# The conversion phase of a fused attention and two-MLP kernel: 298 steps in another order, 20 of them with another engine or pass

## Chip, core and metric

One NeuronCore of a Trainium2 chip runs the whole program. The metric is the device time of one execution in microseconds, the median of the runs shown. The engines are PE (TensorE: matmuls, and PEld, its weight loads), DVE (VectorE), ACT (ScalarE), POOL (GpSimd) and SP (SyncE, which here only issues DMAs). Each takes its instructions in order.

## What is computed

The reference, cut to what matters:

```python
# q, k, v: (8, 8, 576, 64), p: (8, 8, 32, 64), all float32
def sm_attn(qq, kk, vv):
    s = scale * qq @ kk.T; s -= max(s); a = exp(s); return (a / sum(a)) @ vv
p_packed = sm_attn(p, k, v)                 # 32 packed queries per head
x = sm_attn(q, p_packed, p_packed)          # back to 576 tokens per head
x = x.transpose(0, 2, 1, 3).reshape(4608, 512)
h = x @ w_in;  x = (h * sigmoid(1.702 * h)) @ w_out          # 512 -> 2048 -> 512
g = x @ w_gate; x = (g * sigmoid(g) * (x @ w_val)) @ w_out2  # 512 -> 1536 -> 512
```

The five weight matrices arrive as 64-bit floats; everything else is 32-bit. The result has to keep the accuracy of 32-bit floats, so matmul operands are split into a high part and a rest (type fp32r), and each product is three matmuls (`mm3`: high by high, high by rest, rest by high).

## The kernel before

The work goes batch by batch. In each batch the attention's second product is folded into the first MLP: `do_z` multiplies the packed values by `w_in` into `z`, `p1` (L216 through `mm3`, `h<-a,z`) multiplies `z` by the attention weights `a2`, `act1` and `act2` apply the activation and split its result into `gh`, and `p2` (`acc<-gh,wo`) multiplies by `w_out`. One unit is one of 16 column blocks of one half batch: `p1 n`, `act1 n`, `act2 n`, `p2 n`. There are 256 units. After them comes the second MLP.

The change is in the first 19 units. There the weights of the first MLP have to be converted too: 16 blocks of `w_in` (`in 0` to `in 15`) and 16 of `w_out` (`out 0` to `out 15`), each 128 x 512. One block goes through these steps:

- `stage` (L282): SP issues the DMA of a block's 64-bit words, 512 KB, into a buffer that later holds a converted block, so it has to wait until that buffer is free.
- `rebias` (L188): ACT reads the high words as floats and rescales them into `f` (tile `w32`, three buffers).
- `to_f32` (L193): a first pass takes the top bits of the low words into `c` (ACT, L197), and two DVE passes (L199, L201) put sign, exponent and mantissa together. Both read two tensors from SBUF.
- `split_w` or `split_out` (L478, L304, by `split` at L204): ACT rounds to the high part (L205), then POOL or DVE subtracts it from the whole (L206), which frees `f`. The engine is the step's last word; without one it is POOL. `split_w` then has ACT issue a DMA that stores the block to `win`, from where later batches load it. Its buffers are of tag `wh` (three), or, for odd blocks above 4, of tag `raw` (three), which the loads of q and k (`load_raw`) use too.

`do_z n` needs two blocks of `w_in`, `p2` of unit n the block `out` n (modulo 16).

The order in which all this is issued is the text `FIRST` (L19): 298 steps, parted by semicolons, with batch 0's attention (`do_T`, `sc1`, `max1`, `exp1`, `norm1`, `a1T`, `pv`, `do_D`, `sc2`, `max2`, `exp2`, `norm2`, and `split_*` of their results) and, marked `+`, the start of batch 1's. `issue` (L851) calls one function per step. The framework in which the kernel is written takes this order as priority: an engine's instructions may leave it where something later is ready earlier. From unit 19 on a loop issues `p1`, `act2`, `act1`, `p2` of each unit, and the texts `SECOND` and `STEADY` what stands between.

Of the kernel before, what the change touches and what calls it, by code (L numbers as in the profile page):

```python
# [19 lines left out]
    load_raw 0; load_p 0; stage in 0; make_consts; load_raw 1; stage in 2; stage in 1; load_raw 2; load_v 0 0;  # L20
    stage in 3; load_v 0 1; do_p; split_p; do_T 0 0; split_T 0 0; do_T 0 1; split_T 0 1 dve; rebias in 0;
    do_T 1 0; do_T 1 1; sc1 0; load_raw 3; to_f32 in 0; stage in 5; rebias in 2; max1 0; exp1 0; rebias in 1;
    split_T 1 0 dve; split_T 1 1 dve; split_w 0 dve; stage in 4; sc1 1; max1 1; exp1 1; do_T 2 0; do_T 2 1;
    norm1 0; a1T 0; to_f32 in 1; rebias in 3; stage out 0; to_f32 in 2; split_w 2 dve; split_T 2 0 dve;
    copy_a1T 0; split_w 1 dve; pv 0; norm1 1; do_D 0; split_F 0; split_D 0; rebias in 5; to_f32 in 3; split_T 2 1; a1T 1;
    do_T 3 0; stage out 1; rebias out 0; do_T 3 1; split_T 3 0 dve; split_T 3 1 dve; to_f32 in 5; split_w 3;
    stage in 7; copy_a1T 1; sc2 0 0; rebias in 4; to_f32 out 0; pv 1; do_D 1 act; split_F 1; split_D 1; max2 0 0; sc2 1 0;
    exp2 0 0; norm2 0 0; split_w 5 dve; split_a2 0 0; max2 1 0; do_z 0; exp2 1 0; norm2 1 0; stage in 6;
    split_a2 1 0 dve; do_z 1; to_f32 in 4; stage in 8; rebias out 1; split_w 4; stage out 2; to_f32 out 1;
    split_out 0; p1 0; act1 0; rebias in 7; rebias in 6; split_out 1; stage in 13; sc2 0 1; do_z 2; stage in 9;  # L30
    p1 1; act2 0 pool; to_f32 in 7; max2 0 1; split_w 7; sc2 1 1; act1 1; stage out 12; rebias out 2;
    to_f32 in 6; exp2 0 1; norm2 0 1; stage out 3; to_f32 out 2; rebias in 8; split_w 6; stage in 10; do_z 3;
    p1 2; act2 1; stage out 4; rebias in 9; act1 2; rebias out 4; split_out 2; split_a2 0 1; stage in 11;
    to_f32 in 8; max2 1 1; exp2 1 1; rebias out 3; to_f32 in 9; p1 3; split_w 8; stage in 15; rebias in 10;
    to_f32 out 4; act2 2 pool; act1 3; split_out 4 dve; p2 0; split_w 9; stage in 12; to_f32 out 3; do_z 4;
    to_f32 in 10; split_out 3; p1 5; act2 3 pool; rebias in 11; p1 4; act1 4; act1 5; rebias in 13; norm2 1 1;
    p2 1; to_f32 in 11; rebias in 15; split_w 10; stage out 5; split_w 11; to_f32 in 13; do_z 5; stage in 14;
    to_f32 in 15; split_a2 1 1 dve; act2 4 pool; rebias in 12; p2 2; to_f32 in 12; stage out 6; rebias out 5;
    split_w 15; p1 6; act2 5; split_w 12; load_v 1 1; stage out 7; p2 3; to_f32 out 5; rebias in 14; split_w 13;
    act1 6; do_z 6; p1 7; rebias out 7; load_p 1; split_out 5 dve; to_f32 in 14; stage out 8; act2 6 pool;  # L40
    act1 7; rebias out 6; rebias out 8; split_w 14; p1 9; p2 5; p1 8; load_v 1 0; to_f32 out 6; do_z 7;
    stage out 9; act2 7; act1 8; stage out 10; to_f32 out 7; stage out 11; rebias out 12; split_out 6 dve;
    rebias out 9; to_f32 out 8; to_f32 out 9; rebias out 10; to_f32 out 12; p2 4; p2 6; stage out 13;
# [66 lines left out]
def kernel(  # L110
# [856 lines left out]
```

## Time and profile before

| | |
|---|---|
| median of 3 runs | 1714.39 us (1714.21 to 1720.82) |
| profiled execution | 1722.94 us |
| its span, first to last instruction | 1721.2 us |
| PE busy | 1645.1 us (96%) |
| DVE busy | 1209.8 us (70%) |
| ACT busy | 777.3 us (45%) |
| POOL busy | 309.5 us (18%) |
| mean granted TensorE clock | 0.977 |

A row of the profile names the engine, the line of the kernel, the operation and out<-in by the program's tile names, with buffer numbers left out. `<-` after a bracket or between two names is "waited for". Since `split` is a helper, its ACT cast is always L205 and its subtraction L206; the tile tells them apart (`wh`: blocks of `w_in`; `wo`: of `w_out`; `gh`: a unit's activation; `a`: attention weights).

### The profile page before, as it was taken

Reading aid. Unit: us, or ns where it says so; the run is one execution under the profiler, and the core shown is the slowest. Engines: PE = TensorE matmul, PEld = TensorE weight load, DVE = VectorE, ACT = ScalarE, POOL = GpSimd, SP = SyncE. Lnnn points to the kernel's source line nnn. Section 1 sums busy time; section 2 is a strip of 40 time slices with the busy share of each in tenths; the row PEclk is TensorE's granted clock in tenths of the full one; section 3 lists DMA queues with packets and bytes.
Section 4 is the critical chain, followed back from the end, with each engine's and each line's share of the span. In section 5 each row is a group of like instructions: output and inputs, shape, how many; then the busy total and the mean of one; then the engine's idle time right before and its main releaser. Section 6 shows DMA issues by size and latency. Waiting matters only on the chain.

```text
span 1721.2 us, 25917 instructions
## 1 busy us (share of the span) xinstructions
PE 1645.1 (96%) x9264; PEld 1465.1 (85%) x9264; DVE 1209.8 (70%) x2268; ACT 777.3 (45%) x1611; POOL 309.5 (18%) x252
## 2 busy tenths in 40 slices
PE   5678999999999999999999999999999999999998
PEld 4558899998999899999998888888888888888887
DVE  6887978887787977878589555674658466756662
ACT  4675656656465565656455322242224222322222
POOL 1444313222131221302012111000100001001010
PEclk7789999999999999999999999999999999999999
DMA  8864665646466563624388754443445354425411
GB/s 237 266 233 123 197 200 179 218 147 209 129 199 185 163 225 117 212 74 163 125 290 301 265 174 137 163 147 124 157 145 166 95 176 155 154 80 165 157 49 49
DMA packets 169344, 290.59 MB, mean 169 GB/s; under 512 B 54784, under 2 KB 96768, under 8 KB 169216
## 3 DMA queue, kind: packets, MB, share of 16 engines
q1 hardware_dynamic: 165760, 280.03, 50.5%
q10 hardware_dynamic: 3456, 8.91, 1.4%
q8 instruction: 73, 1.20, 0.3%
q14 instruction: 55, 0.45, 0.1%
HBM read 230.16 MB, written 58.72 MB: 168 GB/s over the span
## 4 chain that ended last, share of the span: by engine, by line
PE 73%; DVE 7%; issue 7%; DMA 3%; ACT 2%; POOL 2%; SPq 0%; DVEq 0%; POOLq 0%; ACTq 0%
PE acc L216 31%; PE gv L216 29%; PE h L216 8%; PE pv L400 2%; PE sc L216 2%; PE zp L504 2%; DVE z L507 2%; DMA wh<-win 2%; DVE gh L206 1%; DVE g L554 1%; POOL wo L206 1%; DVE T L335 0%; DMA x<-x2d 0%; PE a1T L383 0%; POOL Th L206 0%
## 5 line engine op out<-in xcount | busy, mean ns | idle before, releaser
L216 PE MATMUL gv<-xh,w 128*128 128x512 f32 x2304 | 554.5, 389 | 0.0
L216 PEld LDWEIGHTS gv<-xh,w 128*128 128x128 f32 x2304 | 432.4, 188 | 89.7
L216 PE MATMUL acc<-gh,wo 128*128 128x288 f32 x3072 | 463.8, 299 | 12.7 <-POOL wo L206 3.1
L216 PEld LDWEIGHTS acc<-gh,wo 128*128 128x128 f32 x3072 | 432.1, 192 | 17.8 <-POOL wo L206 4.0
L216 PE MATMUL acc<-wo,gh 128*128 128x512 f32 x1296 | 326.9, 389 | 0.4
L216 PEld LDWEIGHTS acc<-wo,gh 128*128 128x128 f32 x1296 | 243.0, 188 | 52.1 <-DVE c L210 1.7
L216 PE MATMUL h<-a,z 128*128 128x288 f32 x1536 | 257.0, 301 | 6.2 <-DVE g L554 3.4
L206 DVE TENSOR_TENSOR gh<-g,gh 128x288 fp32r<-128x288 f32 (+1 forms) x293 | 181.2, 618 | 88.6 <-ACT gh L205 87.1
L216 PEld LDWEIGHTS h<-a,z 128*128 128x128 f32 x1536 | 227.1, 193 | 16.5 <-DVE g L554 5.7
L205 ACT CAST gh<-g 128x288 fp32r<-128x288 f32 (+1 forms) x304 | 140.2, 462 | 178.8 <-DVE g L554 130.5
L206 POOL TENSOR_TENSOR gh<-s,gh 128x512 fp32r<-128x512 f32 x60 | 83.0, 1384 | 699.4 <-ACT gh L205 644.7
L798 DVE TENSOR_TENSOR c<-gv,c 128x512 f32<-128x512 f32 x192 | 132.3, 689 | 84.0 <-ACT tb L813 56.6
L205 ACT CAST gh<-s 128x512 fp32r<-128x512 f32 x60 | 37.3, 621 | 247.3 <-DVE s L809 229.5
L552 ACT ACTIVATE sig<-h 128x288 f32<-128x288 f32 x256 | 104.5, 409 | 94.9 <-PE h L216 91.8
L554 DVE SCALAR_TENSOR_TENSOR g<-sig,h 128x288 f32<-128x288 f32 x256 | 114.0, 446 | 36.3 <-ACT sig L552 33.3
L798 DVE TENSOR_TENSOR ta<-gv,c 128x512 f32<-128x512 f32 x96 | 66.2, 689 | 83.1 <-PE gv L216 83.1
L509 POOL TENSOR_TENSOR z<-z,z 128x512 fp32r<-128x512 f32 x56 | 74.7, 1335 | 178.0 <-ACT z L508 178.0
L507 DVE TENSOR_TENSOR z<-zp,z 64x512 f32<-64x512 f32 x112 | 77.0, 688 | 22.5 <-ACT z L506 19.2
L504 PE MATMUL zp<-wh,E 128*128 128x512 f32 x224 | 67.3, 409 | 16.2 <-DMA wh<-win 9.7
L818 ACT ACTIVATE s<-c 128x512 f32<-128x512 f32 x48 | 30.4, 633 | 95.9 <-DVE c L798 95.9
L506 ACT COPY z<-zp 64x512 f32<-64x512 f32 x112 | 65.2, 582 | 14.3 <-PE zp L504 12.1
L206 POOL TENSOR_TENSOR Th<-T,Th 128x576 fp32r<-128x576 f32 x30 | 46.0, 1543 | 126.3 <-ACT Th L205 125.3
(128 smaller groups left out, 1610.0 us busy)
## 6 DMA issues: line engine op xcount, KB each, us to landing
w<-w2s SPq DMA_DIRECT2D x144, 512.0 KB, 3.3
wh<-win SPq DMA_DIRECT2D x112, 512.0 KB, 4.3
w2s<-w SPq DMA_DIRECT2D x36, 512.0 KB, 3.8
w<-w2s SPq DMA_DIRECT2D x48, 256.0 KB, 2.7
raw<-in_k_dram SPq DMA_DIRECT2D x64, 144.0 KB, 3.7
raw<-in_q_dram SPq DMA_DIRECT2D x64, 144.0 KB, 3.7
x2d<-x SPq DMA_DIRECT2D x16, 576.0 KB, 3.8
w2d<-f SPq DMA_DIRECT2D x36, 256.0 KB, 3.2
```

Source lines behind the costliest of these rows:

```text
L205: ACT.copy(dst[:, 0], src)
L206: eng.tensor_tensor(out=dst[:, 1], in0=src, in1=dst[:, 0].bitcast(F32), op=ALU.subtract)
L216: PE.matmul(o, lhsT=lhs(a), rhs=rhs(c), start=first and n == 0, stop=last and n == 2)
L400: PE.matmul(ps[:, c].rearrange("p h i -> p (h i)"), lhsT=vv[:n, k, 2 * c:2 * c + 2].rearrange("p h d -> p (h d)"), rhs=st["a1T", g][:n, k, ...
L504: PE.matmul(ps, lhsT=E[:, c].rearrange("p a i -> p (a i)"), rhs=w[c][:, d], start=d == 0, stop=d == 1)
L506: ACT.copy(x[o], ps[r])
L507: DVE.tensor_tensor(out=x[o], in0=ps[o], in1=x[o], op=ALU.add)
L509: POOL.tensor_tensor(out=y[:, 1], in0=x, in1=y[:, 0].bitcast(F32), op=ALU.subtract)
L552: ACT.activation(s, ps[:, :HS], AF.Tanh, scale=0.5 * 1.702)
L554: DVE.scalar_tensor_tensor(out=g, in0=s, scalar=1.0, in1=ps[:, :HS], op0=ALU.add, op1=ALU.mult)
L798: DVE.tensor_tensor(out=o, in0=ps, in1=c, op=ALU.add)
L818: ACT.activation(s2, c2, AF.Tanh, scale=0.5)
```

## The change

The text `FIRST` is replaced. It holds the same 298 steps in another order, and 20 of them name another engine:

- from POOL to DVE: `split_w` 3, 9, 11, 12, 13, 14; `split_out` 1, 9, 13, 14; `act2` 0, 4, 6;
- from DVE to POOL: `act2` 1 and `split_a2 1 0`;
- the first pass of `to_f32` from ACT to DVE: `in` 2, 11, 14, 15 and `out` 0.

For the last of these `to_f32` gets an engine: on DVE the first pass is a logical right shift of the low word by 29. Of the steps that move furthest: `load_p 0` goes ahead of `load_raw 0`; `stage out 3` goes 21 steps ahead, `stage in 12` 21, `p1 8` 18 (ahead of `do_z 6`), `load_raw 4` 14, `load_raw 5` 9, `+do_p` 20, `+do_T 0 0` 21, `+do_T 1 0` 19; `load_v 1 0` goes 21 back, `p1 12` 18, `p2 6` 13. The texts `SECOND` and `STEADY` and all that follows stay.

The diff:

```diff
@@ -17,39 +17,40 @@
 
 
 FIRST = """
-    load_raw 0; load_p 0; stage in 0; make_consts; load_raw 1; stage in 2; stage in 1; load_raw 2; load_v 0 0;
-    stage in 3; load_v 0 1; do_p; split_p; do_T 0 0; split_T 0 0; do_T 0 1; split_T 0 1 dve; rebias in 0;
-    do_T 1 0; do_T 1 1; sc1 0; load_raw 3; to_f32 in 0; stage in 5; rebias in 2; max1 0; exp1 0; rebias in 1;
-    split_T 1 0 dve; split_T 1 1 dve; split_w 0 dve; stage in 4; sc1 1; max1 1; exp1 1; do_T 2 0; do_T 2 1;
-    norm1 0; a1T 0; to_f32 in 1; rebias in 3; stage out 0; to_f32 in 2; split_w 2 dve; split_T 2 0 dve;
-    copy_a1T 0; split_w 1 dve; pv 0; norm1 1; do_D 0; split_F 0; split_D 0; rebias in 5; to_f32 in 3; split_T 2 1; a1T 1;
-    do_T 3 0; stage out 1; rebias out 0; do_T 3 1; split_T 3 0 dve; split_T 3 1 dve; to_f32 in 5; split_w 3;
-    stage in 7; copy_a1T 1; sc2 0 0; rebias in 4; to_f32 out 0; pv 1; do_D 1 act; split_F 1; split_D 1; max2 0 0; sc2 1 0;
-    exp2 0 0; norm2 0 0; split_w 5 dve; split_a2 0 0; max2 1 0; do_z 0; exp2 1 0; norm2 1 0; stage in 6;
-    split_a2 1 0 dve; do_z 1; to_f32 in 4; stage in 8; rebias out 1; split_w 4; stage out 2; to_f32 out 1;
-    split_out 0; p1 0; act1 0; rebias in 7; rebias in 6; split_out 1; stage in 13; sc2 0 1; do_z 2; stage in 9;
-    p1 1; act2 0 pool; to_f32 in 7; max2 0 1; split_w 7; sc2 1 1; act1 1; stage out 12; rebias out 2;
-    to_f32 in 6; exp2 0 1; norm2 0 1; stage out 3; to_f32 out 2; rebias in 8; split_w 6; stage in 10; do_z 3;
-    p1 2; act2 1; stage out 4; rebias in 9; act1 2; rebias out 4; split_out 2; split_a2 0 1; stage in 11;
-    to_f32 in 8; max2 1 1; exp2 1 1; rebias out 3; to_f32 in 9; p1 3; split_w 8; stage in 15; rebias in 10;
-    to_f32 out 4; act2 2 pool; act1 3; split_out 4 dve; p2 0; split_w 9; stage in 12; to_f32 out 3; do_z 4;
-    to_f32 in 10; split_out 3; p1 5; act2 3 pool; rebias in 11; p1 4; act1 4; act1 5; rebias in 13; norm2 1 1;
-    p2 1; to_f32 in 11; rebias in 15; split_w 10; stage out 5; split_w 11; to_f32 in 13; do_z 5; stage in 14;
-    to_f32 in 15; split_a2 1 1 dve; act2 4 pool; rebias in 12; p2 2; to_f32 in 12; stage out 6; rebias out 5;
-    split_w 15; p1 6; act2 5; split_w 12; load_v 1 1; stage out 7; p2 3; to_f32 out 5; rebias in 14; split_w 13;
-    act1 6; do_z 6; p1 7; rebias out 7; load_p 1; split_out 5 dve; to_f32 in 14; stage out 8; act2 6 pool;
-    act1 7; rebias out 6; rebias out 8; split_w 14; p1 9; p2 5; p1 8; load_v 1 0; to_f32 out 6; do_z 7;
-    stage out 9; act2 7; act1 8; stage out 10; to_f32 out 7; stage out 11; rebias out 12; split_out 6 dve;
-    rebias out 9; to_f32 out 8; to_f32 out 9; rebias out 10; to_f32 out 12; p2 4; p2 6; stage out 13;
-    split_out 8; act1 9; act2 8 pool; split_out 9; split_out 12 dve; p1 10; to_f32 out 10; split_out 10;
-    stage out 14; p1 12; act1 10; rebias out 11; to_f32 out 11; act2 9 pool; act2 10; load_raw 4; split_out 11;
-    split_out 7; p2 7; p1 11; rebias out 14; act1 11; rebias out 13; load_raw 5; load_raw 6; to_f32 out 13;
-    act2 11 pool; stage out 15; act1 12; to_f32 out 14; split_out 13; rebias out 15; split_out 14; p2 8;
-    act2 12 pool; p2 9; p1 13; p2 10; act1 13; +do_p; act2 13; p1 14; act1 14; p2 11; +p_ahead; +do_T 0 0;
-    +split_p; to_f32 out 15; split_out 15 dve; +do_T 0 1; +split_T 0 0; p1 15; act1 15; p2 12; +split_T 0 1 dve;
-    +do_T 1 0; p1 16; act2 15 pool; +sc1 0; +do_T 1 1; p2 13; act2 14 pool; +max1 0; +raw_ahead 0; +exp1 0;
-    +split_T 1 0; p1 17; act1 16; +split_T 1 1; act1 17; p2 14; act2 16; +norm1 0; p1 18; act2 17; act1 18;
-    p2 15; +raw_ahead 1; +sc1 1
+    load_p 0; load_raw 0; stage in 0; load_raw 1; do_T 0 0; make_consts; stage in 2; stage in 1; load_raw 2;
+    load_v 0 0; stage in 3; load_v 0 1; do_p; split_p; split_T 0 0; do_T 0 1; rebias in 0; split_T 0 1 dve;
+    do_T 1 0; do_T 1 1; sc1 0; load_raw 3; to_f32 in 0; do_T 2 0; split_T 1 0 dve; stage in 5; max1 0;
+    split_T 1 1 dve; exp1 0; rebias in 2; rebias in 1; sc1 1; max1 1; norm1 0; split_w 0 dve; stage in 4;
+    exp1 1; do_T 2 1; to_f32 in 1; a1T 0; rebias in 3; to_f32 in 2 dve; split_w 2 dve; split_w 1 dve;
+    to_f32 in 3; copy_a1T 0; stage out 0; pv 0; norm1 1; do_D 0; split_D 0; split_T 2 0 dve; rebias in 5;
+    split_F 0; a1T 1; stage in 7; split_T 2 1; do_T 3 0; stage out 1; do_T 3 1; split_T 3 0 dve; sc2 0 0;
+    rebias out 0; split_w 3 dve; rebias in 4; to_f32 in 5; split_T 3 1 dve; copy_a1T 1; max2 0 0;
+    to_f32 out 0 dve; pv 1; do_D 1 act; split_w 5 dve; split_D 1; sc2 1 0; exp2 0 0; norm2 0 0; split_a2 0 0;
+    split_F 1; max2 1 0; do_z 0; exp2 1 0; norm2 1 0; stage out 2; stage in 6; to_f32 in 4; rebias out 1;
+    do_z 1; stage in 8; split_w 4; split_out 0; split_a2 1 0; to_f32 out 1; stage out 3; p1 0; act1 0;
+    rebias in 7; split_out 1 dve; sc2 0 1; stage in 13; do_z 2; stage in 9; p1 1; to_f32 in 7; rebias out 3;
+    max2 0 1; rebias in 6; split_w 7; act2 0; act1 1; to_f32 in 6; rebias out 2; exp2 0 1; sc2 1 1;
+    to_f32 out 2; rebias in 8; norm2 0 1; rebias in 9; split_w 6; stage in 10; p1 2; stage out 12; stage out 4;
+    stage in 12; do_z 3; act1 2; rebias out 4; split_out 2; rebias in 10; split_a2 0 1; act2 1 pool; max2 1 1;
+    stage in 11; p1 3; exp2 1 1; to_f32 in 8; to_f32 in 9; split_w 8; to_f32 out 4; stage in 15;
+    split_out 4 dve; act1 3; act2 2 pool; p2 0; p1 5; to_f32 out 3; split_w 9 dve; do_z 4; to_f32 in 10;
+    rebias in 11; rebias in 13; p1 4; act1 4; act2 3 pool; split_out 3; norm2 1 1; act1 5; rebias in 15;
+    stage out 5; to_f32 in 11 dve; split_a2 1 1 dve; to_f32 in 15 dve; split_w 10; to_f32 in 13; p2 1;
+    split_w 11 dve; do_z 5; p2 2; act2 4; stage in 14; stage out 6; stage out 7; rebias in 12; to_f32 in 12;
+    load_v 1 1; split_w 15; p1 6; rebias out 5; act2 5; split_w 12 dve; to_f32 out 5; p1 8; split_w 13 dve;
+    act1 6; rebias in 14; p2 3; to_f32 in 14 dve; do_z 6; load_p 1; rebias out 6; split_out 5 dve; p1 7;
+    stage out 8; act2 6; p1 9; rebias out 7; act1 7; rebias out 8; split_w 14 dve; p2 5; do_z 7; rebias out 12;
+    to_f32 out 7; stage out 9; act2 7; to_f32 out 6; act1 8; stage out 10; stage out 11; act1 9; rebias out 9;
+    split_out 6 dve; to_f32 out 8; rebias out 10; to_f32 out 9; p2 4; to_f32 out 12; stage out 13; split_out 8;
+    split_out 9 dve; load_raw 4; load_v 1 0; act2 8 pool; split_out 12 dve; p1 10; to_f32 out 10; split_out 10;
+    stage out 14; act1 10; rebias out 11; p2 6; to_f32 out 11; act2 9 pool; load_raw 5; act2 10; split_out 7;
+    split_out 11; p2 7; +do_p; p1 11; act1 11; rebias out 14; rebias out 13; +do_T 0 0; act2 11 pool;
+    to_f32 out 13; p1 12; act1 12; stage out 15; to_f32 out 14; load_raw 6; p2 8; split_out 13 dve; p1 13;
+    rebias out 15; +do_T 1 0; split_out 14 dve; p2 9; act1 13; p2 10; act2 12 pool; act2 13; p1 14; act1 14;
+    +p_ahead; +split_p; p1 15; to_f32 out 15; +do_T 0 1; split_out 15 dve; +split_T 0 0; act1 15; p2 11; p2 12;
+    +split_T 0 1 dve; p1 16; act2 15 pool; +do_T 1 1; +sc1 0; p2 13; +raw_ahead 0; act1 16; act2 14 pool;
+    +max1 0; +raw_ahead 1; +exp1 0; p1 18; +split_T 1 0; p1 17; act1 17; p2 14; act2 16; +norm1 0; +split_T 1 1;
+    act2 17; p2 15; act1 18; +sc1 1
...
@@ -190,12 +191,15 @@
         ACT.activation(f, w64[key][:, :, 1].bitcast(F32), AF.Copy, scale=2.0 ** -112)
         wf[key] = f
 
-    def to_f32(key):
+    def to_f32(key, eng=ACT):
         w, w32[key] = w64.pop(key), wf.pop(key)
         f = w32[key].bitcast(I32)
         c = at.tile([P, 512], I32, tag="wc", bufs=2, name="wc")
-        ACT.activation(c, w.bitcast(U16).rearrange("p c (two h) -> p c two h", h=2)[:, :, 0, 1], AF.Copy,
-                       scale=2.0 ** -13, bias=2.0 ** -15 - 0.5)
+        if eng is ACT:
+            ACT.activation(c, w.bitcast(U16).rearrange("p c (two h) -> p c two h", h=2)[:, :, 0, 1], AF.Copy,
+                           scale=2.0 ** -13, bias=2.0 ** -15 - 0.5)
+        else:
+            DVE.tensor_scalar(out=c, in0=w[:, :, 0], scalar1=29, scalar2=None, op0=ALU.logical_shift_right)
         DVE.scalar_tensor_tensor(out=c, in0=f, scalar=3, in1=c,
                                  op0=ALU.logical_shift_left, op1=ALU.bitwise_or)
         DVE.scalar_tensor_tensor(out=f, in0=f, scalar=-0x80000000, in1=c,
@@ -855,7 +859,7 @@
             f(*[int(c) if c.isdigit() else engines.get(c, c) for c in a])
 
     ops = dict(attention(0), load_p=load_p, load_raw=load_raw, load_v=load_v, make_consts=make_consts, stage=stage,
-               rebias=lambda *k: rebias(k), to_f32=lambda *k: to_f32(k), split_out=split_out, p1=u_p1, act1=u_act1,
+               rebias=lambda *k: rebias(k), to_f32=lambda kind, j, eng=ACT: to_f32((kind, j), eng), split_out=split_out, p1=u_p1, act1=u_act1,
                act2=lambda n, eng=DVE: act2(units[n], eng), p2=lambda n: p2(units[n]))
     second = attention(1)
     issue(FIRST, ops, second)
```

## Rows read from the trace of the kernel before

**Rows 1.** the page's slices of PE, 40 of 43.03 us each, busy tenths

```profile
PE   5678999999999999999999999999999999999998
```

**Rows 2.** stretches: length, busy us of PE PEld DVE ACT POOL, PEclk, DMA, GB/s

```profile
0.00:155.00 155.00, 104.66 (x479) 88.89 (x480) 118.75 (x209) 93.14 (x196) 62.98 (x57) 0.79 0.70 217
60.00:155.00 95.00, 71.69 (x362) 62.36 (x361) 77.71 (x120) 63.64 (x132) 49.07 (x37) 0.81 0.61 193
80.00:105.00 25.00, 14.43 (x55) 11.20 (x54) 24.30 (x32) 17.29 (x33) 13.10 (x11) 0.77 0.93 310
155.00:255.00 100.00, 97.18 (x694) 92.85 (x694) 84.58 (x194) 60.28 (x141) 26.48 (x21) 1.00 0.68 201
```

**Rows 3.** PE's timeline, 100 to 170 us: start, us, what, [idle before <-releaser]

```profile
103.45 0.79 PE L216 MATMUL zp<-wh,F 128*128 128x512 f32 x1 [5.36 <-ACT wh L205]
...
153.08 1.76 PE L216 MATMUL sc<-Th,pb 128*128 128x320 f32 x12
```

**Rows 4.** PE's waits, 0 to 155 us: total, times, longest

```profile
PE zp L216 <- ACT wh L205: 7.7, 3, 5.4
PE acc L216 <- POOL wo L206: 3.1, 2, 2.2
...
PE zp L216 <- POOL wh L206: 2.7, 3, 1.1
...
PE sc L216 <- POOL pb L206: 0.6, 1, 0.6
```

**Rows 5.** ACT's waits, 0 to 155 us

```profile
ACT f L190 <- POOL wh L206: 5.2, 6, 1.6
...
ACT f L190 <- DMA w64out<-in_moe_w_out_dram: 1.0, 1, 1.0
```

**Rows 6.** the chain of waits in 0 to 155 us, by line

```profile
by line: issue 7.6%; POOL wh L206 3.4%; POOL wo L206 3.3%; PE acc L216 3.2%; DMA win<-wh 2.6%; DMA raw<-in_k_dram 2.0%; ACT f L190 1.9%; POOL gh L206 1.7%; PE h L216 1.3%; DVE wc L199 1.3%; ACT Th L205 1.2%; POOL pb L206 1.2%; ACT gh L205 1
```

**Rows 7.** groups by form, 0 to 155 us: busy us, mean ns, idle before

```profile
L201 DVE SCALAR_TENSOR_TENSOR f<-f,wc 128x512 int32<-128x512 int32 x32 | 31.4, 984 | 0.8
L199 DVE SCALAR_TENSOR_TENSOR wc<-f,wc 128x512 int32<-128x512 int32 x32 | 26.6, 835 | 4.7 <-ACT f L190 2.4 <-ACT wc L197 2.2
...
L206 POOL TENSOR_TENSOR wh<-f,wh 128x512 fp32r<-128x512 f32 x12 | 18.2, 1516 | 19.9 <-ACT wh L205 17.9 <-issue 1.9
L206 POOL TENSOR_TENSOR wo<-f,wo 128x512 fp32r<-128x512 f32 x11 | 15.8, 1447 | 14.7 <-ACT wo L205 7.8 <-DVE f L201 6.9
...
L206 POOL TENSOR_TENSOR gh<-g,gh 128x288 fp32r<-128x288 f32 x11 | 11.9, 1097 | 14.7 <-ACT gh L205 14.7
...
L197 ACT ACTIVATE wc<-w64in 128x512 int32<-128x512 uint16 x16 | 10.6, 669 | 0.0
...
L206 DVE TENSOR_TENSOR gh<-g,gh 128x288 fp32r<-128x288 f32 x7 | 3.5, 502 | 0.0
...
L206 DVE TENSOR_TENSOR wh<-f,wh 128x512 fp32r<-128x512 f32 x4 | 2.7, 686 | 0.4 <-ACT wh L205 0.4
...
L376 DVE TENSOR_SCALAR a<-a,sm 128x576 f32<-128x576 f32 x3 | 1.6, 519 | 0.1
```

**Rows 8.** DVE's timeline, 80 to 125 us

```profile
83.89 0.30 DVE L320 STREAM_TRANSPOSE pT<-pt 128x128 f32<-128x128 f32 x1
...
103.02 0.68 DVE L199 SCALAR_TENSOR_TENSOR wc<-f,wc 128x512 int32<-128x512 int32 x1
103.80 1.58 DVE L201 SCALAR_TENSOR_TENSOR f<-f,wc 128x512 int32<-128x512 int32 x1
```

**Rows 9.** POOL's timeline, 0 to 165 us

```profile
103.47 3.05 POOL L206 TENSOR_TENSOR wh<-f,wh 128x512 fp32r<-128x512 f32 x2 [1.30 <-ACT wh L205]
```

**Rows 10.** line 201 alone in 80 to 105 us

```profile
80.00:105.00 25.00, 11.30 (x9) 0.77 0.93 310
```

**Rows 11.** line 199 alone in 80 to 105 us

```profile
80.00:105.00 25.00, 8.32 (x9) 0.77 0.93 310
```

**Rows 12.** SP's waits, 0 to 165 us

```profile
SPq L248 <- DMA win<-wh: 11.7, 2, 6.7
```

## The prediction

> **What bounds the kernel now.** First the slices of the page: TensorE (PE) is full in all of its 40 slices but the first four, 172 us of 1721.2, and the last [rows 1]. The reader is to see that the change lies in the first four. Then the stretches [rows 2]: in 0 to 155 us PE is busy 104.66 us, at a granted clock of 0.79 of full; from 155 to 255 us it is busy 97.18 of 100 at full clock. The phase of the text FIRST ends about there: the scores `+sc1 1`, its last step, are on PE at 153.08 us [rows 3]. After it PE sets the time, so what the phase gains or loses is carried to the end nearly one to one.
>
> Inside the phase no engine is full throughout. VectorE (DVE) is the busiest, 118.75 us of 155, and from 80 to 105 us it is full: 24.30 of 25 [rows 2]. Then what PE waits for: at the start for the packed queries p, later for ScalarE's (ACT) and GpSimd's (POOL) casts and splits of weights (7.7, 3.1 and 2.7 us) [rows 4]. The longest hole is 5.36 us before 103.45, in front of a `do_z` product [rows 3]. So the rate is that of converting 32 weight blocks, a loop through ACT, DVE and POOL; the transfers are not what ends last, since ACT waits for landed blocks of `w_out` only 1.0 us, but 5.2 us for POOL's splits of `wh` alone, which free its buffer [rows 5]. Last the chain of waits: POOL's splits are 3.4% and 3.3% of these 155 us, 10.4 us in all, its `gh` splits another 1.7% or 2.6 us [rows 6].
>
> **Engines: the amounts.** Ten wide splits go from POOL to DVE (`split_w` 3, 9, 11 to 14; `split_out` 1, 9, 13, 14). On POOL they take 1.516 and 1.447 us, on DVE 0.686 [rows 7]: POOL loses 6 x 1.516 + 4 x 1.447 = 14.9, DVE gains 6.9. Of the 288-wide ones `act2` 0, 4, 6 go to DVE, `act2` 1 and `split_a2 1 0` to POOL: net one to DVE, +0.5 there and -1.1 on POOL [rows 7]. Five first passes of `to_f32` leave ACT (5 x 0.669 = 3.3 [rows 7]) for a new DVE instruction that the trace does not show. Its nearest rows are DVE's own pass over 128x576 floats by a scalar, 0.519, and the 512-wide integer passes, 0.68 alone [rows 7, 8]; being an integer shift of 512 it is nearer to the second, and I take 0.60: +3.0 (2.6 to 3.4). Sum: DVE +10.4, POOL -16.0, ACT -3.3.
>
> **What comes back on DVE.** The same pass takes 0.68 at 103.02, before a POOL split runs, and 1.58 at 103.80, while two run [rows 8, 9]. So POOL's work is paid twice. Over the phase the 64 combining passes cost 32 x (0.835 - 0.685) + 32 x (0.984 - 0.685) = 14.4 us more than alone [rows 7], that is 0.23 us for each of POOL's 62.98 [rows 2]. From 80 to 105 us the 18 of them take 11.30 + 8.32 = 19.6 [rows 10, 11] where 18 x 0.685 = 12.3 would do: 7.3 us on POOL's 13.10, or 0.56 each. Removing 16.0 us of POOL gives DVE back 3.7 (at 0.23) to 9.0 (at 0.56); its net is +6.7 to +1.4. DVE does not get lighter. What gets shorter is the way of one block through a split: 0.69 for about 1.48.
>
> A rule of the Trainium skill speaks here ("SBUF — State Buffer", section "Who interferes with whom"): VectorE and GpSimd share one port pair, and whichever starts first holds it for the whole instruction, also against a one-input `tensor_scalar` in a two-port mode. The two rows at 103 us agree for two-input passes; for the new first pass no row here shows it. What it would do is the third rival below.
>
> **The sum.** (a) The start: p is now loaded before the keys, so the packed split can be done when the keys land. PE's wait for it behind the first two matmuls is 0.6 [rows 4]: -0.6. (b) POOL's wide splits on the chain: ten of 23 leave, 10.4 x 10/23 = 4.5, and DVE's take 0.686/1.48 of that: -2.4 (0 if DVE is late instead, -4.5 if it hides them). (c) The full stretch 80 to 105: by the text four of the moved splits (9, 11, 12, 13) and three first passes (11, 14, 15) fall in or near it, 4 x 0.686 + 3 x 0.60 = 4.5 on DVE, of which 4 x 1.516 x 0.56 = 3.4 comes back: +1.1 (+4.5 if nothing does). (d) `p1 8` now stands ahead of `do_z 6` and can run in the hole of 5.36 us; twelve matmuls take 1.76 at full clock [rows 3], six 0.9: -0.9 (0 to -5.4, were the hole filled). (e) Two of eleven `gh` splits fewer on POOL, 2.6 x 2/11 x 0.54: -0.3. (f) ACT: its waits for POOL shrink with (b), and 3.3 us of passes leave. That costs and gives nothing while DVE feeds it late; where PE waits for ACT's casts some of it shows. Between 0 and -3.3 I take -1.0, nearer to nothing, because ACT is busy 93.14 of 155 [rows 2]. Sum -4.1.
>
> Costed at nothing: the moved transfers. `stage out 3`, `stage in 12` and `load_raw 4` and 5 go ahead, `load_v 1 0` back by 21 steps. SP issues in order, and behind `load_raw 4`, whose buffer is that of an odd weight split, now stand `load_v 1 0` and `stage out 14`; the two waits of this kind for a store are 11.7 us [rows 12], so these could land some 6 us later. What hides it is how little ACT waits for blocks (1.0 us); if that cover is gone, it costs up to those 6. `+do_p` and two transposes of batch 1 go 19 to 21 steps ahead: nothing, since the framework already runs them far ahead of the text, the transpose of p at 83.89 us [rows 8] though it is step 259 of 298.
>
> The profiled execution took 1722.9, 8.5 above the median of 1714.39. I carry the difference: 1722.9 - 4.1 = 1718.8 for that one, 1714.4 - 4.1 = 1710.3, so 1710 for the median. About 0.5% (8.6 us) is what a measurement of this kernel can tell from no change; the forecast lies inside it.
>
> **The rivals.** 1. The holes close. From 60 to 155 us PE is idle 95 - 71.69 = 23.3 us [rows 2]. If the new order takes half of that away, -11.7 and the start's -0.6 give 1702. For it: the holes are ends of chains through POOL, and the faster splits stand in most of them. Against: DVE has no room in 80 to 105.
> 2. Slower: DVE becomes the bound. If its idle time in the phase (155 - 118.75 = 36.25) stays and the POOL work that is left meets DVE as often as before, all of +10.4 is on the path: 1724.8. It decides in the stretch from the `split_w 9` to the `split_w 14`; with DVE busy above 129 us in the phase, the phase ends beyond 163. For it: 24.30 of 25. Against: 0.56 us per POOL microsecond ought to come back there.
> 3. The first pass on DVE and POOL hold each other up. The price is that of a combining pass, 1.58 - 0.68 = 0.9, at POOL's share in the full stretch, 13.10/25: 5 x 0.9 x 0.52 = 2.4 on DVE, and POOL's splits that much later. That leaves -1.7: 1712.7.
> 4. The text's order is hardly the chip's: the framework orders by what is ready (batch 1's transpose of p at 83.89). Then only the engines count, -2.4 + 1.1 - 0.3 = -1.6: 1712.8.
>
> **How the numbers follow.** Forecast 0.34, of which 0.04 ends beyond 8.6 us faster; holes close 0.31; DVE bound 0.17; port 0.08; engines alone 0.10. Faster by over 0.5%: 0.31 + 0.04 = 0.35. Within: 0.30 + 0.08 + 0.10 = 0.48. Slower: 0.17. The range: below, the first rival with three quarters of the idle time taken instead of half (-17.5 - 0.6, 1696); above, the second at its price (1725). Outside each end I leave a tenth. The forecast's own range is 1704 to 1716: (b), (c), (d) and (f) between their ends, not all at once.
>
> **What would show it.** Right: POOL busy some 47 us in the phase instead of 63, the combining passes' means lower, DVE busy 120 to 126, PE's waits for POOL's `wo` and `wh` about halved, no 5.4 us hole before a `do_z`, `+sc1 1` some 4 us before 153. Wrong to the fast side: PE's idle from 60 us to the end of the phase halved, or its clock at the upper of its two levels (2.4 GHz, rows at 1.00) before 140 us. Wrong to the slow side: DVE over 129 us, or a first pass of more than 0.7 us beside POOL, or ACT waiting several microseconds for a landed block.

## The result and the profile after

The changed kernel took 1701.96 us (median of 6 runs, 1697.84 to 1705.4) where the kernel before took 1716.52 in runs on the same chip: a ratio of 0.9913 [0.9894, 0.9931], 14.6 us or 0.9% faster. In a later comparison it was 1704.21 against 1718.69 (0.9923 [0.9897, 0.9948]). The forecast of 1710 moved the right way by less than a third of that; the time is inside the whole range, below the forecast's own (1704 to 1716), and it is the one that the first rival gave (1702).

**Where the time went.** Three marks of PE's timeline part the program. The first is the first full row of batch 1's `pv` product, a few microseconds behind the phase. Before:

```profile
163.28 2.76 PE L400 MATMUL pv<-a1T,vt 128*128 128x64 f32 x20
...
898.10 12.20 PE L216 MATMUL gv<-xh,w 128*128 128x512 f32 x53
```

After:

```profile
149.96 2.76 PE L404 MATMUL pv<-a1T,vt 128*128 128x64 f32 x20
...
877.00 16.49 PE L220 MATMUL gv<-xh,w 128*128 128x512 f32 x72
```

The reader is to see three pieces: up to `pv` 163.3 and 150.0 us, from there to the second MLP (`gv`) 734.8 and 727.0, and from `gv` to the end of the execution (1722.94 and 1701.60) 824.8 and 824.6. The first piece is what the change touches: -13.3 us, which is the change of the medians but for about one microsecond. The last is fixed. The middle one, seven batches, varied from 727 to 740 us over the fourteen profiles of this study, since a single batch took anything from 98.3 to 104.0 us; the changed kernel itself showed 727.0 in one profile and 733.3 in another. So below every kernel is compared by its median and by the time of this `pv` row, called the mark. It repeated within 0.5 us for the changed kernel (149.96, 149.45).

The stretches of [rows 2] in the changed kernel (length, busy us and count of PE PEld DVE ACT POOL, PEclk, DMA, GB/s), the last line up to the end of `+sc1 1`:

```profile
0.00:155.00 155.00, 111.02 (x571) 95.40 (x572) 128.30 (x254) 96.39 (x208) 48.02 (x48) 0.93 0.74 233
60.00:155.00 95.00, 78.32 (x456) 68.41 (x455) 85.00 (x160) 66.62 (x144) 34.41 (x27) 0.91 0.68 214
80.00:105.00 25.00, 17.18 (x59) 13.20 (x60) 22.51 (x40) 18.41 (x36) 4.82 (x3) 0.73 0.96 330
155.00:255.00 100.00, 98.17 (x702) 94.23 (x702) 86.05 (x201) 61.52 (x142) 25.18 (x21) 1.00 0.64 189
...
0.00:142.35 142.35, 98.56 (x478) 83.52 (x479) 118.23 (x225) 90.51 (x191) 46.50 (x46) 0.93 0.74 237
```

And the kernel before up to the end of its `+sc1 1` ([rows 3]: 153.08 + 1.76):

```profile
0.00:154.84 154.84, 104.50 (x478) 88.73 (x479) 118.59 (x209) 92.98 (x196) 62.98 (x57) 0.79 0.70 217
```

This pair is the reading that matters. Both do the same 478 matmuls; DVE has 16 instructions more (ten splits, five first passes, and net one of the 288-wide splits), POOL 11 fewer, ACT 5 fewer, as the change says. Yet DVE is busy 118.23 us instead of 118.59: as much came back as was moved to it. And the 12.5 us by which the phase is shorter are two things: PE is idle 43.8 us instead of 50.3 (-6.5), and its matmuls are busy 98.56 instead of 104.50 (-5.9). The matmuls themselves got shorter (a trace models their ends, so the split is a rough one). Nearly all of that lies behind 60 us, and the granted clock goes with it. From 60 us to the end of the phase, before:

```profile
60.00:154.84 94.84, 71.53 (x361) 62.20 (x360) 77.55 (x120) 63.48 (x132) 49.07 (x37) 0.81 0.61 194
```

and after:

```profile
60.00:142.35 82.35, 65.87 (x363) 56.52 (x362) 74.93 (x131) 60.74 (x127) 32.90 (x25) 0.89 0.67 218
```

As the clock has two levels, 0.50 and 1.00, these shares stand for some 36 us at the lower one before and 18 after (an estimate: twice 0.19 of 94.84 and twice 0.11 of 82.35). The matmuls in this stretch take 71.53 and 65.87 us. The clock figures from 0 us on, 0.79 and 0.93, can't be set side by side; the last section says why. The groups by form show which matmuls got shorter, `acc` and `zp` above all, before:

```profile
L216 PE MATMUL acc<-gh,wo 128*128 128x288 f32 x192 | 38.5, 346 | 11.8 <-POOL wo L206 3.1 <-DVE gh L206 2.9 <-ACT wo L205 2.1
...
L216 PE MATMUL zp<-wh,F 128*128 128x512 f32 x48 | 21.6, 566 | 10.5 <-ACT wh L205 7.7 <-POOL wh L206 2.7
```

and after:

```profile
L220 PE MATMUL acc<-gh,wo 128*128 128x288 f32 x192 | 34.1, 327 | 4.9 <-ACT wo L209 2.0 <-DVE wo L210 1.5 <-POOL wo L210 1.1
...
L220 PE MATMUL zp<-wh,F 128*128 128x512 f32 x48 | 19.1, 509 | 10.0 <-POOL wh L210 3.1 <-ACT wh L209 3.1 <-DVE wh L210 2.0
```

With the same 192 and 48 matmuls, `acc` is 4.4 us shorter and its idle time 6.9; `zp` is 2.5 us shorter.

Where DVE's time came from is in the groups by form, 0 to 155 us (busy us, mean ns, idle before):

```profile
L205 DVE SCALAR_TENSOR_TENSOR f<-f,wc 128x512 int32<-128x512 int32 x32 | 27.6, 864 | 0.2
L203 DVE SCALAR_TENSOR_TENSOR wc<-f,wc 128x512 int32<-128x512 int32 x32 | 24.5, 769 | 2.1 <-ACT wc L199 1.8
L210 POOL TENSOR_TENSOR wo<-f,wo 128x512 fp32r<-128x512 f32 x7 | 10.2, 1459 | 18.7 <-ACT wo L209 16.8 <-PE h L220 1.3 <-DVE f L205 0.6
...
L210 POOL TENSOR_TENSOR wh<-f,wh 128x512 fp32r<-128x512 f32 x6 | 9.4, 1564 | 10.8 <-ACT wh L209 10.8
...
L210 DVE TENSOR_TENSOR wo<-f,wo 128x512 fp32r<-128x512 f32 x9 | 7.2, 807 | 0.3 <-ACT wo L209 0.3
L210 DVE TENSOR_TENSOR wh<-f,wh 128x512 fp32r<-128x512 f32 x10 | 6.8, 684 | 0.0
...
L202 DVE TENSOR_SCALAR wc<-w64in 128x512 int32<-128x512 int32 x4 | 1.7, 418 | 0.0
```

The 64 combining passes take 52.1 us instead of 58.0 [rows 7]; the new first pass takes 0.42 us, not 0.60. What PE waits for in the phase [rows 4] (total us, times, longest):

```profile
PE sc L220 <- ACT Th L209: 17.5, 4, 7.8
...
PE zp L220 <- POOL wh L210: 3.1, 3, 1.6
PE zp L220 <- ACT wh L209: 3.1, 2, 1.6
...
PE acc L220 <- POOL wo L210: 1.1, 2, 1.0
```

The waits for ACT's casts of `wh` fell from 7.7 to 3.1 us, those for POOL's `wo` from 3.1 to 1.1; those for POOL's `wh` did not fall (2.7, 3.1). PE's timeline answers [rows 3]:

```profile
7.75 0.85 PE L220 MATMUL sc<-Th,pb 128*128 128x320 f32 x2 [7.75 <-ACT Th L209]
...
17.56 3.56 PE L220 MATMUL sc<-Th,pb 128*128 128x320 f32 x12 [5.55 <-ACT Th L209]
...
96.08 0.50 PE L220 MATMUL zp<-wh,F 128*128 128x512 f32 x1 [1.58 <-ACT wh L209]
...
134.12 1.75 PE L220 MATMUL acc<-gh,wo 128*128 128x288 f32 x12
...
140.60 1.75 PE L220 MATMUL sc<-Th,pb 128*128 128x320 f32 x12
```

`+sc1 1` starts at 140.60 instead of 153.08. In front of `do_z 6` stands a hole of 1.58 us where 5.36 stood. And in its last 12 us before the end of the phase PE has no hole, at the upper level of its clock. The same stretch before:

```profile
131.44 2.29 PE L216 MATMUL acc<-gh,wo 128*128 128x288 f32 x8 [2.23 <-POOL wo L206]
133.53 1.40 PE L216 MATMUL h<-a,z 128*128 128x288 f32 x5
134.73 2.87 PE L216 MATMUL acc<-gh,wo 128*128 128x288 f32 x12
```

There PE waits 2.23 us for a POOL split of `wo`, and behind it twelve matmuls take 2.87 us where the changed kernel has 1.75. PE ran these at the lower level of its clock:

```profile
131.44:137.20 5.76, 5.76 (x24) 5.76 (x25) 2.64 (x3) 3.70 (x8) 4.39 (x4) 0.50 0.48 143
```

So the time lost here is more than the hole's own length. The windows over 130 to 142.35 us say the same, before:

```profile
130.00:142.35 12.35, 10.91 (x62) 10.87 (x63) 7.34 (x11) 6.68 (x14) 7.33 (x6) 0.72 0.23 68
```

and after:

```profile
130.00:142.35 12.35, 12.35 (x95) 12.26 (x94) 10.67 (x25) 8.62 (x22) 5.03 (x4) 1.00 0.17 40
```

### The profile page after: what moved, and what is told of

Same layout as the page of the kernel before. It is cut to its first block, busy times and chain, and to the rows that moved or that the text cites. A ratio compares the mean times of both kernels' runs of the same rounds, so it can differ in the third digit from the quotient of the medians.

```text
span 1699.9 us, 25897 instructions
## 1 busy us (share of the span) xinstructions
PE 1633.9 (96%) x9264; PEld 1455.7 (86%) x9264; DVE 1208.0 (71%) x2284; ACT 773.8 (46%) x1606; POOL 291.6 (17%) x241
## 4 chain that ended last, share of the span: by engine, by line
PE 81%; DVE 8%; issue 4%; DMA 3%; ACT 2%; POOL 1%; SPq 0%; ACTq 0%; DVEq 0%; POOLq 0%
PE acc L220 34%; PE gv L220 29%; PE h L220 9%; PE sc L220 3%; PE pv L404 3%; PE zp L508 2%; DVE z L511 1%; DMA wh<-win 1%; DVE gh L210 1%; DVE g L558 1%; DVE f L205 1%; PE a1T L387 1%; DVE wc L203 0%; ACT z L510 0%; DMA w64in<-in_moe_w_in_dram 0%
## 5 line engine op out<-in xcount | busy, mean ns | idle before, releaser
L220 PE MATMUL acc<-gh,wo 128*128 128x288 f32 x3072 | 457.8, 297 | 5.9 <-ACT wo L209 2.0
L220 PEld LDWEIGHTS acc<-gh,wo 128*128 128x128 f32 x3072 | 427.4, 190 | 10.3 <-ACT wo L209 2.9
L220 PEld LDWEIGHTS acc<-wo,gh 128*128 128x128 f32 x1296 | 243.0, 188 | 52.1 <-DVE c L214 1.7
L220 PE MATMUL h<-a,z 128*128 128x288 f32 x1536 | 253.6, 299 | 7.6 <-DVE g L558 6.0
L220 PEld LDWEIGHTS h<-a,z 128*128 128x128 f32 x1536 | 223.6, 191 | 18.0 <-DVE g L558 9.3
```

Source lines behind the costliest of these rows:

```text
L220: PE.matmul(o, lhsT=lhs(a), rhs=rhs(c), start=first and n == 0, stop=last and n == 2)
```

## The experiments

All kernels below compute the whole result; one adds work on top. One thing limits all but that one: a changed word in the text changes also the order into which the framework puts every engine's instructions, so "one part undone" is that part and what the reordering does with it. In the table, "before" is the kernel before in the same comparison.

| kernel | median us (runs) | before | ratio | mark | to before / after |
|---|---|---|---|---|---|
| before | | 1716.5 to 1718.7 | | 163.28 | / +13.3 |
| changed kernel | 1701.96 (6) | 1716.52 | 0.9913 [0.9894, 0.9931] | 149.96 | -13.3 / |
| changed, again | 1704.21 (4) | 1718.69 | 0.9923 [0.9897, 0.9948] | 149.45 | -13.8 / -0.5 |
| order alone | 1715.62 (10) | 1718.09 | 0.9984 [0.997, 0.9999] | 156.49 | -6.8 / +6.5 |
| engines alone | 1709.13 (4) | 1718.09 | 0.994 [0.9925, 0.9955] | 155.46 | -7.8 / +5.5 |
| first passes back | 1712.2 (10) | 1718.09 | 0.9963 [0.9951, 0.9974] | 152.83 | / +2.9 |
| splits back | 1718.49 (10) | 1718.09 | 1.0001 [0.9991, 1.0011] | 160.71 | / +10.8 |
| POOL kept busy | 1708.32 (4) | 1718.69 | 0.9947 [0.9927, 0.9966] | 153.11 | / +3.2 |
| splits alone | 1714.75 (10) | 1718.69 | 0.9981 [0.9969, 0.9993] | 159.62 | -3.7 / |
| early order | 1705.93 (5) | 1718.69 | 0.9935 [0.9915, 0.9956] | 152.47 | / +2.5 |
| passes alone | 1716.83 (10) | 1717.7 | 0.9997 [0.9979, 1.0015] | 162.07 | -1.2 / |
| six more splits | 1705.53 (5) | 1717.7 | 0.993 [0.9905, 0.9955] | 150.67 | / +0.7 |
| all splits | 1704.2 (4) | 1717.7 | 0.9922 [0.9894, 0.995] | 149.47 | / -0.5 |
| more passes | 1710.86 (10) | 1717.7 | 0.9958 [0.9942, 0.9974] | 155.93 | / +6.0 |

**Order and engines parted.** The first has the new order with the old engine words, the second the old order with the 20 new ones:

```diff
# order alone, against the changed text (two of the 20 words)
-split_w 9 dve; to_f32 in 11 dve
+split_w 9; to_f32 in 11
# engines alone, against the text before (two of the 20 words)
-split_w 9; to_f32 in 11
+split_w 9 dve; to_f32 in 11 dve
```

> The new order with all 20 engine choices of the kernel before. Theory A (the engines: fewer POOL splits shorten the conversion loop and give DVE time back): little is left, 1713 to 1717 us, last step of the phase on PE near 152 us. Theory B (the order closes the holes, whatever the engines): 1702 to 1706, last step near 141 to 144. Theory C (the order was made for these engines, either alone is worth little or less than nothing): 1714 to 1722.

> The order of the kernel before with the 20 new engine choices. Theory A: 1702 to 1706 us, POOL busy 48 us in the first 155, the combining passes at 0.77 and 0.86 us as in the changed kernel. Theory B: 1713 to 1717. Theory C: 1714 to 1722, as DVE gets 10.4 us more where it was full already.

By the mark the order is worth 6.8 us and the engines 7.8; the sum, 14.6, is 0.8 to 1.3 more than the two together give. So by the mark they are nearly independent, and neither is small. The medians agree for the engines (9.0 us), but give the order alone only 2.5 us, barely clear of noise; its phase is shorter, and the batches behind it took longer in it (see what stays open). No theory fits both runs: the order's median is in the ranges of A and C, but its last step is on PE at 145.88 us, earlier than A's 152; the engines alone end between A's range and B's.

With the order alone POOL keeps its 62.94 us and the combining passes their sum (893 and 900 ns where 984 and 835 stood): the order gained without touching the contention. Both keep a hole of 4 us before `do_z 6`, although the text of the order alone has `p1 8` ahead of it. Order alone, PE's timeline:

```profile
98.98 0.79 PE L218 MATMUL zp<-wh,F 128*128 128x512 f32 x1 [3.96 <-ACT wh L207]
```

Engines alone:

```profile
100.62 0.80 PE L218 MATMUL zp<-wh,F 128*128 128x512 f32 x1 [4.34 <-ACT wh L207]
```

It closes to 1.58 only with both. Engines alone, the stretch up to the end of `+sc1 1`:

```profile
0.00:147.51 147.51, 96.72 (x478) 80.80 (x479) 121.60 (x225) 90.31 (x191) 47.74 (x46) 0.92 0.73 228
```

PE is idle 50.8 us here, as long as before (50.3), and all that this phase is shorter is in the matmuls: 96.72 us for 104.50. So shorter matmuls do not need a smaller sum of holes.

**The parts of the engines undone.**

```diff
# first passes back, against the changed text, for in 2, 11, 14, 15 and out 0
-to_f32 in 11 dve
+to_f32 in 11
# splits back, for split_w 3, 9, 11 to 14 and split_out 1, 9, 13, 14
-split_w 9 dve
+split_w 9
```

> The changed kernel with the five first passes of to_f32 back on ACT. If the passes matter, 1705 to 1709 us; if they only trade 0.67 us of ACT for 0.42 of DVE off the path (theories A and B alike), 1701 to 1704. In theory C every engine choice counts: 1705 or more.

> The changed kernel with the ten wide splits back on POOL. Theory A puts the gain here: 1711 to 1716 us, the combining passes longer again (0.83 and 0.98 us). Theory B: 1703 to 1706. Theory C: above 1710.

The ten splits carry most of it: without them the mark is 10.8 us later and the median is that of the kernel before, even above the 1711 to 1716 that theory A expected. The first passes are worth 2.9 us by the mark. The median gives 8 to 10 us, and at 1712.2 it is above the 1705 to 1709 expected if the passes matter; the difference is again behind the phase. With the splits back on POOL, the stretch up to the end of `+sc1 1`, the same 478 matmuls:

```profile
0.00:151.91 151.91, 103.75 (x478) 86.84 (x479) 124.16 (x214) 90.07 (x190) 62.86 (x56) 0.88 0.72 222
```

DVE has 11 instructions fewer than in the changed kernel and is 5.9 us busier (124.16, 118.23), with POOL busy 16.4 us more. And the phase's 9.6 us more are again both things: PE's matmuls are 5.2 us longer (103.75, 98.56), its idle time 4.4 us (48.2, 43.8).

**How much of this is contention alone.** The next run takes the changed kernel and gives POOL seven subtractions over 128 x 512 floats that nothing reads, behind `split_w` 3, 9, 11 to 14 and `split_out 1`. They read the high part just written and write a spare tile, so no step's own work gets longer; PE, DVE, ACT and SP keep their order of instructions.

```diff
+    def extra(dst):
+        x = dst[:, 0].bitcast(F32)
+        junk = at.tile([P, 2, 2 * G * P], F32R, tag="pb", name="junk").bitcast(F32)
+        POOL.tensor_tensor(out=junk[:, 0], in0=x, in1=x, op=ALU.subtract)
...
             split(y, w32.pop(("in", j)), eng)
+            if j in (3, 9, 11, 12, 13, 14):
+                extra(y)
```

> The changed kernel itself, for comparison with the others of this call. All theories: 1700 to 1705 us, last step of the phase on PE near 141 us, the next batch's first product with v near 150.

> The changed kernel with seven extra POOL subtractions of 128x512, one behind each of split_w 3, 9, 11 to 14 and split_out 1, of the high part by itself into a spare tile that nothing reads; the order of PE, DVE, ACT and SP is that of the changed kernel to the instruction. Only POOL's use of SBUF comes back, the blocks' way stays short. Theory A1 (what the moved splits gave is DVE time, by less contention): DVE's passes lengthen by some 7 x 0.85 = 6 us, 1707 to 1711 us. Theory A2 (the gain is the shorter way of a block through its split): 1701 to 1705, though DVE's passes are longer.

```profile
L204 DVE SCALAR_TENSOR_TENSOR f<-f,wc 128x512 int32<-128x512 int32 x32 | 29.4, 920 | 0.2
L202 DVE SCALAR_TENSOR_TENSOR wc<-f,wc 128x512 int32<-128x512 int32 x32 | 26.1, 818 | 1.9 <-ACT wc L198 1.7
```

The time, 1708.3 us against 1704.2 for the changed kernel in the same comparison, is in the range of theory A1, though the passes lengthen by less than its 6 us: 8.8 us more on POOL make the 64 passes 3.4 us longer (55.5, 52.1) and put the mark 3.2 to 3.7 us later: 0.36 to 0.42 us for each of POOL's microseconds. Up to the end of `+sc1 1`, with the same 225 instructions, DVE is 6.0 us busier (124.19, 118.23), and PE's matmuls take as long as in the changed kernel (98.29, 98.56); here all of the delay is idle time:

```profile
0.00:145.51 145.51, 98.29 (x478) 82.14 (x479) 124.19 (x225) 90.71 (x191) 55.38 (x53) 0.92 0.74 231
```

The extra work also stands in POOL's queue, ahead of POOL's own splits. But PE's waits for POOL's `wh` and `wo` do not grow (2.8 and 1.0 us, for 3.1 and 1.1); those for DVE's splits of `wh` do (4.7, for 2.0). Over the 14.9 us that the ten splits took on POOL that is some 6 us of their 10.8 (an estimate from these two runs). The rest is what else a split on DVE does, such as the shorter way of its block; that part was not measured by itself.

**In the old order, and half of the new one.**

```diff
# splits alone, against the text before (ten such words)
-split_w 9
+split_w 9 dve
# passes alone, against the text before (five such words)
-to_f32 in 11
+to_f32 in 11 dve
# early order: the changed text's first 125 steps, through do_z 3, then the other steps in the order before,
# all with the new engines
```

> The kernel before with only the ten wide splits moved to DVE. The engines alone gave 9 us together with the passes and the small splits. Theory A (the splits): 1708 to 1711 us. If the passes carried it: 1714 to 1718. By theory C (parts that only work together) no gain either, 1715 or more.

> The kernel before with only the five first passes on DVE. The splits alone brought batch 1's first product with v from 163.3 to 159.6 us, all 20 to 155.5. If the passes carry the rest (theory A): near 159, 1713 to 1715 us. If the five small splits or the joint order carry it: 162 to 164, 1716 to 1720.

> The first 125 steps of the new order (through do_z 3), then the other 173 in the order of the kernel before, all with the new engines. If the new order earns its part early (do_z 2 and 3 come 3 us sooner than in the engines-only kernel): 1703 to 1706 us, next batch's first product with v near 151. If it earns it late, with p1 8 ahead of do_z 6 and batch 1's start: 1708 to 1711, near 155.

In the old order the splits are worth 3.7 us and the passes 1.2 at the mark; nothing of the latter shows in the median. So the splits are worth less than half there of what they are worth in the new order: POOL falls as far (49.42 us), but the hole behind a cast of `wh` grows to 6.9 us. The early order gets 3.0 of the 5.5 us that the new order adds to the engines alone, so about half of its worth lies ahead of `do_z 3`. Which step brings it stays open. Against the expectations: the splits alone, at 1714.75, miss the 1708 to 1711 of theory A; the passes alone fall where the small splits or the joint order carry the rest; the early order's median is in the range for "early", its mark between the two.

In the early order one first pass ran beside POOL's split. DVE's timeline:

```profile
87.10 0.68 DVE L204 SCALAR_TENSOR_TENSOR f<-f,wc 128x512 int32<-128x512 int32 x1
87.81 1.40 DVE L201 TENSOR_SCALAR wc<-w64in 128x512 int32<-128x512 int32 x1
```

and POOL's:

```profile
87.26 1.66 POOL L209 TENSOR_TENSOR wh<-f,wh 128x512 fp32r<-128x512 f32 x1 [1.36 <-issue]
```

POOL started at 87.26 and ended at 88.92; the pass, 0.42 us elsewhere, ended at 89.21. It reads one tensor, and still it ended only after POOL had. Three more first passes were stretched so, one with the engines alone (0.81 us) and two with more passes (1.51, 0.90); all four ended 0.28 to 0.29 us after the split on POOL. Where the pass starts first it keeps its length. In the changed kernel one first pass on DVE

```profile
83.92 0.43 DVE L202 TENSOR_SCALAR wc<-w64in 128x512 int32<-128x512 int32 x1
```

met a split on POOL that began 0.08 us later:

```profile
84.00 1.48 POOL L210 TENSOR_TENSOR wo<-f,wo 128x512 fp32r<-128x512 f32 x1 [5.80 <-ACT wo L209]
```

**Beyond the change.** Three runs go further along the same lines: the other six `split_w` of `w_in` to DVE; all 13 wide splits that POOL has left; or eight first passes more (`in` 8, 9, 10, 12, 13, `out` 4, 5, 6).

```diff
# six more splits
-split_w 10
+split_w 10 dve
# all splits: those six, and
-split_out 3
+split_out 3 dve
# more passes
-to_f32 in 10
+to_f32 in 10 dve
```

> The changed kernel with its other six split_w on DVE too. By the price found with extra POOL reads (0.4 us of DVE per microsecond of POOL) the exchange costs DVE 6 x (0.69 - 1.5 x 0.4) = 0.5 us and makes six blocks' way 0.8 shorter. Theory A: a further gain of 1 to 4 us, 1700 to 1703, the product with v at 146 to 149. If DVE is the bound by now: 1704 to 1708.

> The changed kernel with all 13 wide splits that POOL still has on DVE: POOL busy near 29 us in the phase, DVE's passes near 0.72. Theory A with no limit: 1697 to 1702 us. If DVE is the bound by now (9 us more work, some 7 back): 1704 to 1710.

> The changed kernel with eight more first passes on DVE (in 8, 9, 10, 12, 13, out 4, 5, 6): DVE +3.4 us at 0.42 each, ACT -5.4. If the five passes gained because ACT's queue was in front of DVE's passes, more of them gain more: 1700 to 1703, DVE's waits for ACT's first pass gone. If DVE is the bound: 1705 to 1709.

The splits' worth is used up: with six or 13 splits fewer on POOL the mark stays at 150.7 and 149.5, and neither median differs from the changed kernel's. The further gain that theory A expected did not come. All splits, the combining passes by form in 0 to 155 us:

```profile
L204 DVE SCALAR_TENSOR_TENSOR f<-f,wc 128x512 int32<-128x512 int32 x32 | 24.2, 762 | 0.0
L202 DVE SCALAR_TENSOR_TENSOR wc<-f,wc 128x512 int32<-128x512 int32 x32 | 24.2, 760 | 1.2 <-ACT f L190 0.5 <-ACT wc L198 0.5
```

and the stretch up to the end of `+sc1 1`:

```profile
0.00:141.91 141.91, 97.40 (x478) 82.41 (x479) 120.81 (x237) 90.52 (x190) 28.32 (x33) 0.92 0.79 245
```

The passes still shrink (48.4 us for 52.1), but not by enough any more: DVE is 2.6 us busier than in the changed kernel. That the shorter way of the 13 blocks is no longer what the phase waits for is argued, not shown. DVE's idle time up to the end of `+sc1 1`, 36.3 us before, is 24.1 in the changed kernel and 21.1 here. Eight more first passes cost 6.0 us at the mark. Up to the end of their `+sc1 1`:

```profile
0.00:148.30 148.30, 101.74 (x477) 87.58 (x478) 123.37 (x233) 86.64 (x183) 49.05 (x46) 0.87 0.75 231
```

and in DVE's timeline one of its first passes, stretched from 0.42 us:

```profile
73.08 1.51 DVE L201 TENSOR_SCALAR wc<-w64in 128x512 int32<-128x512 int32 x1
```

DVE has 5.1 us more than in the changed kernel, POOL 2.5 more, ACT 3.9 less, and the phase ends 5.9 us later. So these eight passes, 3.4 us at 0.42 each, cost 6 us by the mark, while the first five, which take nothing from POOL either, gained 2.9. The median, 1710.86, lies just beyond what the expectation gave for DVE as the bound. None of these beats the changed kernel.

## Why the prediction was right in its direction and too small

**What held.** The change acts in the phase and is carried on nearly one to one; POOL fell by 16.5 us (16.0 predicted); the stretch from 80 to 105 us was relieved; the passes' means fell; PE's waits for POOL's `wo` fell from 3.1 to 1.1 us and the hole before `do_z 6` to 1.58. The waits for POOL's `wh`, which were to be halved as well, did not fall (2.7, 3.1). The cover for the moved transfers held: ACT's longest wait for a landed block is 1.9 us.

**The step that failed** is the sum's idea that the gain is the sum of PE's waits that go away, each at its own length. Half of the 12.5 us is PE's matmuls being shorter (104.50 to 98.56). The prediction had a faster PE only in its list of signs "to the fast side", with no term in the sum. That sign came true: from 105.3 to 142.35 us the clock is at 1.00 throughout, where the kernel before shows 0.80. Term by term:

- (b) Splits on the chain, -2.4 taken, -4.5 at most: -3.7 measured in the old order, -10.8 in the new. Undersized: besides the shorter way of a block it holds the passes that POOL no longer stretches (some 6 us of the 10.8). Seen from PE, 5.2 us of it are matmuls, whose clock from 60 us to the end of the phase is 0.83 with the splits back on POOL and 0.89 without.
- (c) DVE in the full stretch, +1.1: the wrong sign. In that window DVE is 24.30 us busy before and 22.51 after (with other work in it), and over the phase -0.4 where +1.4 to +6.7 stood. The first pass at 0.42 for 0.60 gave 0.9 of it, and the passes returned 5.9 of the 3.7 to 9.0 expected. Those two would leave +3.6; the other 4.0 lie outside the passes and were not traced.
- (a) and (d), the order: -1.5 together, and the fourth rival held that the text's order hardly counts. It counts for 6.8 us by the mark, 2.5 in the median. (a) itself was worth nothing: the first scores start 0.7 us earlier, the second ones at 17.56 for 17.48. (d) was the wrong reason: `p1 8` did not fill the hole. In both kernels 48 matmuls of `h<-a,z`, eight units, run ahead of `do_z 6`, and the order alone leaves 3.96 us of it.
- (f) First passes off ACT, -1.0, at most -3.3: 2.9 in the new order by the mark, so near the far end; 1.2 in the old.
- (e) was not tried by itself.

**The rivals.** The first, the holes close, has the right time by half of the right cause, so in part by luck: PE's idle time from 60 to 155 us went from 23.3 to 16.7 us, less than a third and not half, and faster matmuls made up for it. The second, DVE the bound, decided nothing here, since its conditions were false: DVE's passes got shorter, and its idle time in the phase fell from 36.3 to 24.1 us. Eight more first passes made DVE and the phase longer, as that rival would have it. The third needs a first pass that starts behind a POOL split; none of the five in the changed kernel did (0.41 to 0.43 us each). In the early order one did and took 1.40 us. There the rule weighed in the prediction (the Trainium skill, "SBUF — State Buffer", section "Who interferes with whom": of VectorE in a two-port mode and GpSimd, the one that issues first gets the shared port pair for the whole instruction) agrees with the rows, in both orders of start, also for an instruction with one tensor input. Whether the pass ran in such a mode no row here shows.

**What stays open.** Order alone and first passes back lose 4 to 5 us more in the median than their marks say: their medians less mark less 824.6 leave 734.5 and 734.8 us for the seven batches, and splits back 733.2, where the eleven other rows leave 727 to 731. The text that orders that stretch is the same in all; why these three take longer in it was not found.

Nor is it shown that the longer matmuls come from the holes. That they go with the clock is read in the traces: from 60 us to the end of the phase PE's matmuls take 69.8 to 71.5 us in the four with a clock of 0.81 to 0.83 (before, splits back, passes alone, more passes) and 64.1 to 66.8 in the ten others, at 0.84 to 0.91. With PE's total idle time they do not go: the engines alone leave it as it was and have short matmuls, and POOL kept busy adds 3.4 us of it and no longer matmuls. What in the pattern of PE's work brings the lower level about was not tried by a run of its own.

## What to carry to other kernels

Where two engines hold each other up, price a move by busy time up to a fixed mark in both kernels, with the same work inside: ten splits and five passes cost DVE no busy time here, as two-input passes that POOL had stretched became shorter. Look at TensorE's holes and at its granted clock apart: the shorter matmuls were worth as much here as the shorter holes, and with the engines alone they were all of the gain. And stop where the return stops: with POOL at 48 us of the phase further splits gave nothing, and eight more passes on the busiest engine lost 6 us of the 13 gained.

## What the chip showed that was not expected

A logical shift of 512 integers per partition, read at every second word, took DVE 0.42 us; the combining passes over as many, with two tensors read, take 0.68 alone. Behind a POOL split the one took up to 1.51. With more passes, two of them ran at 0.41 us inside a POOL split of 3.63 us; that split had started 0.2 us behind one on DVE and was itself the stretched one.

The granted clock of a row can stand at 1.00 where the trace has no record of the clock. The second row of batch 0's `pv`, 18 matmuls, took 4.51 us in both kernels; the clock over it was 0.50 before:

```profile
26.79:31.30 4.51, 4.50 (x19) 3.96 (x18) 1.74 (x3) 1.33 (x2) 1.41 (x1) 0.50 0.79 263
```

and 1.00 after:

```profile
27.47:31.98 4.51, 4.51 (x19) 3.97 (x18) 1.14 (x2) 1.09 (x2) 1.40 (x1) 1.00 0.72 239
```

But in the second profile of the changed kernel, with the same instructions in the same order, it is 0.50 again:

```profile
27.23:31.74 4.51, 4.51 (x19) 3.97 (x18) 1.15 (x2) 1.09 (x2) 1.40 (x1) 0.50 0.72 237
```

The clock records of that trace begin at 21.0 us and those of the kernel before at 21.2; those of the changed kernel's first trace begin at 50.6. So its 1.00 before that is no reading, and the rise from 0.79 to 0.93 over the phase is partly this: the second profile has 0.83 up to the end of its phase. From 60 us on, where all three have records, the figures can be compared: 0.81 before, 0.89 and 0.88 in the changed kernel.
